# Two 16-point steps in sixteen 32x32 tiles, the second branch in column halves, and a new instruction order, in a one-core spectral filter kernel

## Chip, core and metric

The kernel runs on one core of one Trainium2 chip. Its time is the device time of one execution in microseconds (us); the figure compared is the median over runs. Five engines take part: TensorE (PE in the profile, its weight loads PEld), VectorE (DVE), ScalarE (ACT), GpSimd (POOL) and SyncE (SP). In this kernel the last two do nothing but start DMA transfers.

## The reference: what is computed

Two branches A and B filter the same input `x` of shape (2048, 1024) in the frequency domain and are mixed row by row by a gate:

```python
x = A_x
g = sigmoid((x * gate_w).sum(-1, keepdims=True))
def branch(w_r, w_i):
    X = rfft2(x.astype(float32), axes=(-2, -1))      # 2048 rows, 1024 columns -> 513
    return irfft2(X * (w_r + 1j * w_i), s=(S, D)).astype(bfloat16)
return g * branch(A_w_r, A_w_i) + (1 - g) * branch(B_w_r, B_w_i)
```

Inputs and output are bfloat16. The forward transform is shared; the product with the weights and the way back exist once for each branch (b = 0 and b = 1).

## The kernel before, in words

The 2048-point transform of the rows is split into 128 x 16. All steps are matmuls with constant matrices, their results are copied from PSUM to bfloat16 in SBUF ("evicted") by ACT or DVE, and real symmetry is used throughout. Stage by stage, with the names that the code gives to its nodes:

- **Load.** `x` comes in eight transfers of 512 KB (two of the 16 row residues `n2` each), with the matrix `F` (512 KB), then `DM` and `SK`, all from SP.
- **fS, fT, S1, Z** (`xrows`, `stage_s1`, `stage_s1f`). DVE folds columns (sum and difference of mirrored halves), PE applies the 128-point step for each residue (8 matmuls 128x256), ACT or DVE evicts to `TV`. For the residues in `FOLD2` (10 to 15) DVE folds a second time (`f2`) and the matmuls are 128x128.
- **D, Q** (`stage_d`). The column transform: 16 steps of 8 matmuls 128x256, evicted to `RING`. Every D reads all sixteen Z.
- **S2, X** (`stage_s2`). The 16-point step on the rows. The work is cut in four quarters `sq`; one S2 is 16 matmuls in four 64x64 tiles of the array (64 rows of weights by 64 columns). Evicted to `R4`.
- **mul** (`prod`). The products with the weights: 32 DVE operations, all on 128x2052 elements. Weights come through the POOL queue.
- **I, V, turn** (`stage_i1`, `stage_iw`). The inverse 16-point step: 16 stages of 32 matmuls in 64x64 tiles (`WIDE`) or 64 matmuls in 64x32 tiles. Each stage gives two tiles V of 128x1024, and each V is moved across partitions by a DMA of 256 KB (`turn`), SBUF to SBUF, from a cell of the buffer `RING` to `TV`. The cell is free again when the DMA has landed.
- **S1A, S1B, S1H, G** (`s1inv`). The inverse 128-point step of both branches, the gate folded into its matrices (`RA`, `RB`): 16 matmuls 128x128 for each residue.
- **Di, o, u, e, y, out** (`tail`). The inverse column step, and DVE folds back: `u` (only for the pairs in `FOLD3`: 0, 2, 4, 6), `e`, `y`; then the output goes out from SP in pairs of residues.

The order of the work is fixed ahead: the nodes are numbered as the code creates them, and the string `ORDER` lists them in base 36, two characters each; `ENGS` names the engine of each entry (p, a, d, g for POOL, s for SP), `CELLS` the buffer cells. `Plan.replay` reads them, and each engine executes its own nodes in that order. Each engine waits on semaphores only for what its next node needs (`Sched`). In the order before, SP's first nodes are x rows 0-1, `F`, x rows 2-3 to 14-15, `DM`, `SK`; DVE's first `mul` is the one of quarter 1 after two Q and two X.

All matmuls are issued from line 392, DVE's two-operand work from line 395, evictions from line 417 (ACT) and 418 (DVE), DMAs from line 426, so the profile is read by tensor names and shapes.

Of the kernel before, what the change touches and what calls it, by code (L numbers as in the profile page):

```python
# [4 lines left out]
dt = mybir.dt  # L5
# [5 lines left out]
NS = 513  # L11
# [4 lines left out]
FOLD2 = (10, 12, 14)  # L16
WIDE = ((0, 0), (0, 1), (0, 2), (0, 3), (1, 3))
EARLY = (0, 1, 2, 3)
FOLD3 = (0, 2, 4, 6)
PAIRS = {"warm": 12, "S2": 16, "I1": 64, "I1W": 32, "S25": 8, "gate": 8, "zg": 4, "gm": 8}  # L20
DEPTH = ((0, 2), (2, 4), (4, 6), (6, 8), (8, 10), (10, 12), (12, 14), (14, 16))
ORDER = (
    "020b0h030c000i04010506070n0j080m090f0a0g0d0q0s0e0o0t0r0k0y0w0p0z0u0l24140x15100v251b12111a181h131g1c19261o1e1p1d16271q1f"
    "1r2s28171w1s1u1i1t292v1x1v1j2a1z1m2w1k1y2t2b1n1l22202c232u212y2x2z2d3o3m2e3p3b3n2f3s3c2g3q3t372h3r31382i403u3239422j412q"
    "303v3a33352k343w3x362l493z3y2m434a3d5n3g2n445p3e3i2o473h3f45482p5o3j464o5q3k4p4b3l4h4i4j4e4c5b4f4k4d4g4l5w2r5c5r5x635z59"
    "4q5u4m774r5y644n5i605s5v5a5t4y5l4s6v5j5m4t614u4z5k6a6w50624v6d6b4x6e7n4w6c5d6h655e6f5g5f6i55665h516g56676t686j527o696o6m"
    "6u6k6n7z6r6l6x816p6s7l6q726y82706z7m757188737976747p788b8c7a7s897q7t7b808a7r57837c7e7d587f7g86538454877j857u7h7k7i8u7v7x"
    "8d7w8z7y8i908v918j8w8e8k928x8f938l8y8g8m9b94958h979f969c9u8n8o9g9q988q9v9d9r9h9e9w8p9i9s99a59x8r9a9ja99t9k8saia69l8t9yam"
    "aa9z9ma7aja09nabana1aka89oaoac9palava2apazaeawa3b8aqb0a4axadb9arbab1afaybdasbmb2agatbbahbeb4boaubcbibrbhbnb3bsbfbpbgb5bq"
    "bvb6bub7btbjbwbkbxblbybz")  # L30
ENGS = (
    "sadsadpsasssdasdsasaspdspdapdpadpagdadpagdpadpdadpagdpdapgdadpgadppdagpdadgdpapdagdappgdpappagppgdpagpdgpapgapdgpddpagds"
    "ppappgddpagpdagpaddpgadpagpdapagdpapdaaddpadppdapadapsdpadadpapdagdapgagdgpaddagpdaagpdadpadagdagpdpadagdpagpdagdapadgpa"
    "dagdagpdagdgpadasdagpadgspdagdadagpdgsdpadsdgpadadgagpagspadpspgpppapdpappadpapapddadpdapddapddapdpapdapdpadsdpaddpadsdp"
    "addpaddpadpadpdsapdapdadpdaspdadapdapdpaddpsadasadpdadadpddadddsdddddsds")
CELLS = (
    "071052794002440d28404702486402463204060846204g62402640g027420648g02461204260204406624gij7062402062446086002462460284602a"
    "0244668c026042a264680402ac60402046400824264002c406408248a060424c0460280g424078064867c60046")
# [6 lines left out]


def spot(m):
    r = m // 2
    return 32 * (m % 2) + 4 * (r % 8) + r // 8


def make_consts():
# [4 lines left out]
    for j in range(4):  # L57
        for i in range(4):
            for ri in range(2):
                for sq in range(4):  # L60
                    p = 32 * j + 8 * i + 4 * ri + sq
                    slot, at0 = 4 * sq + j % 2 * 2 + i // 2, j // 2 == 0
                    kap[p], img[p] = 32 if slot == 0 and at0 and i % 2 else 64 * (i % 2) + 16 * (j // 2) + slot, ri
# [22 lines left out]
    for par in range(2):  # L86
        for h in range(2):
            l = (2 * (2 * np.arange(128) + h) + par)[:, None]
# [31 lines left out]
    SK = np.zeros((128, 1152))  # L120
    KI = KI.reshape(2, 2, 2, 32, 32)
    for z in range(2):
        lut = []
        for b in range(2):
            for t in range(16):
                lut.append((2 * (2 * t + b),) + ((0, 1, 2 * t + b) if z else (b, 0, 2 * t)))
                lut.append((2 * (2 * t + (b if z else 1 - b)) + 1, 1 if z else b, 0, (2 * t + b) if z else 2 * t + 1))
        for hh in range(2):
            if hh:
                lut = [(4 * t + 2 * b, b, 0, 2 * t) for b in range(2) for t in range(16)] + \  # L130
                      [(4 * t + 2 * (1 - b) + 1, b, 0, 2 * t + 1) for b in range(2) for t in range(16)]
            for m, blk, y, r in lut:
                m = spot(m)
                for t in range(3):
                    SK[64 * hh + 32 * blk:64 * hh + 32 * blk + 32, z * 192 + t * 64 + m] = S2[y, t, :, r]
                for c in range(2):
                    for t, v in enumerate((KI[y, c, 0], -KI[y, c, 0], KI[y, c, 1])):
                        o = 384 + z * 384 + (c * 3 + t) * 64 + 32 * blk
                        for th in range(2):
                            SK[64 * hh + m, o + th:o + 32:2] = v[r].reshape(2, 16)[:, 8 * th:8 * th + 8].ravel()  # L140
# [8 lines left out]
    for i in range(2):  # L149
        M[64 * i:64 * i + 64, 20 + i] = 1.0  # L150
# [142 lines left out]
class Plan:  # L293
# [40 lines left out]
    def emit(self, S):  # L334
        def phys(k):
            if isinstance(k, tuple) and isinstance(k[0], Tile):
                t = k[0]
                a = self.limit[t.pool][0]
# [12 lines left out]
def bass_gated_mix__spectral_gfnet__spectral_gfnet__prompt_kernel(  # L351
# [11 lines left out]
    def ap(t, off, dims, p0=0, np_=128):  # L363
# [7 lines left out]
    SK = sb("SK", 1152)  # L371
# [3 lines left out]
    NCELL = 28  # L375
# [9 lines left out]
             {"ps": ("ps", 4), "p1": ("ps", 8), "st": ("ring", 4), "q": ("ring", 2), "qx": ("ring", 2), "v": ("ring", 14),  # L385
              "o": ("late", 8), "e": ("late", 8), "y": ("ring", 5), "u": ("ring", 5), "w": ("ring", 1)})
    xv = A_x[0].rearrange("(p r) d -> p r d", r=16)
    outv = out[0].rearrange("(p r) d -> p r d", r=16)
    wsrc = {0: (A_w_r, A_w_i), 1: (B_w_r, B_w_i)}

# [6 lines left out]
    def cost(ns):  # L397
        o = sum(max(0.056, n / 2400 + 0.0025) if n > 64 else 0.03 for n in ns)
        return {"pe": (o, o + 0.21)}

    def vt(n):
        return {"dve": (0.07 + 0.00052 * n, 0.205 + 0.00052 * n)}

    def pe(name, ns, build, reads, writes, alloc=(), **kw):
        return P.add(name, cost(ns), lambda e: build(), reads, writes, alloc=alloc, **kw)

    def ev(name, n, io, reads, writes, slow=False, only=None, **kw):
        x = 0.285 if slow else 0.0
        engs = {"act": (0.062 + 0.000833 * n + x, 0.24 + 0.000833 * n + x),
                "dve": (0.075 + 0.00104 * n + 0.08 * (x > 0), 0.22 + 0.00104 * n + 0.08 * (x > 0))}  # L410
        if only:
            engs = {only: engs[only]}

        def build(eng):
            o, i = io()
            if eng == "act":
                return [lambda e: e.activation(o, i, ACT.Copy)]  # L417
            return [lambda e: e.tensor_copy(o, i)]  # L418
        return P.add(name, engs, build, reads, writes, **kw)

    def dma(name, eng, pairs, mb, rate, reads, writes, kind=True, n=1, **kw):
        if not isinstance(eng, str):
            es = {"pool": (0.6, mb / 118 * 1000), "sp": (0.63, mb / 118 * 1000)}
        else:
            es = {eng: (0.6 * n, mb / rate * 1000)}
        n = P.add(name, es, lambda e: [lambda q, d=d, s=s: q.dma_start(d, s) for d, s in pairs()], reads, writes, dma=kind, **kw)  # L426
        n.mb = mb
        return n
# [9 lines left out]
    def cload(eng, t, off, key, a, b, keys, more=(), **kw):  # L438
        dma("c_" + key, eng, lambda: [(ap(t, off, [[1, b - a]]).bitcast(dt.uint16), cst[key].ap()[:, a:b])],
            (b - a) * 256e-6, 400, list(more), keys, **kw)  # L440

    P.add("zero8", {"dve": (0.1, 0.2)}, lambda e: [lambda e: e.memset(ap(G8, 0, [[1, 8]]), 0.0)], [], ["G8"])
    P.add("table", {"act": (1.4, 1.5)}, lambda e: [lambda e: e.activation(ap(ZG, 0, [[1, 8]]), ap(G8, 0, [[1, 8]]), ACT.Sigmoid)],
          ["G8"], ["ZG"])

    def xload(a, b):
        dma("x", "sp", lambda: [(ap(WAB, XO + a * 1024, [[1024, b - a], [1, 1024]]), xv[:, a:b, :])],
            (b - a) * 0.262, 410, [], [("x", i) for i in range(a, b)] + [("xl", a)])
# [5 lines left out]
    dma("gw", "act", lambda: [(ap(GW, 0, [[1, 1024]], 0, 1), gate_w.rearrange("(o d) -> o d", o=1))], 0.002, 400, [], ["gw"])  # L454
    cload("act", MS, 0, "MS", 0, 64, ["MS"])
    cload("sp", DM, 0, "DM", 0, 2048, ["DM"])
    cload("sp", SK, 0, "SK", 0, 1152, ["SK"])

    P.key = ("in", 1)
    pt = pit[id(WAB)]  # L460

    def rows(b, c, p, step, s0, r0, dims):
        src = wsrc[b][c]
        return (AP(WAB, p * pt + (2 * b + c) * WH + s0 * WP, [[step * pt, 32 // step]] + [[WP, d[1]] for d in dims if d[0] < 0] + [[1, dims[-1][1]]]),
                AP(src.tensor, src.offset + r0 * NS, dims))

    def wload(name, key, eng, prs, mb, b):
        dma(name, eng, lambda: prs, mb, 106, [("xl", m) for m in range(0, 8 if name in ("Ws0", "W00") else 14, 2)], [("W", b) + key], after=[("x", m) for m in range(16)] if b else [], n=len(prs))

    wk = {0: [], 1: []}  # L470

    for i, (a, b) in enumerate(((0, 256), (256, 1280))):
        P.key = ("in", 1)
        P.add("FN", {"act": (0.15 + (b - a) * 0.00083, 0.25 + (b - a) * 0.00083)},
# [398 lines left out]
```

## Time and profile before

| what | value |
|---|---|
| median of 3 runs | 126.01 us (125.93 to 126.77) |
| span of the profiled execution | 124.9 us |
| PE, DVE, ACT, POOL busy in the span | 103.4, 99.5, 96.5, 41.6 us |
| DMA moved | 27.85 MB, mean 223 GB/s |
| granted TensorE clock, mean | 0.968 |

The profiled execution has no time of its own beside its span; the 1.1 us between span and median are taken as what lies around it. How to read the views: a timeline row is start, length, engine, source line, operation, output<-input, tile, shape and count, and in brackets the idle time before it and who ended it. A window row gives for each engine the busy us and, in brackets, the instructions in that stretch, then the granted clock, the mean busy share of the 16 DMA engines and GB/s.

### The profile page before, as it was taken

How to read it: one execution, taken by the hardware profiler on the slowest of the kernel's cores; microseconds unless marked ns; L12 is line 12 of the kernel's file. 1: busy time of each engine (PE TensorE's matmuls, PEld its weight loads, DVE VectorE, ACT ScalarE, POOL GpSimd, SP SyncE). 2: the span in 40 equal slices, each digit the busy share in tenths (PEclk: the TensorE clock that was granted, in tenths of full speed). 3: DMA queues.
4: the chain of work that ended last, by engine and by line, in shares of the span. 5: the costliest groups of instructions: out<-in, count | busy, mean ns of one | idle time of the engine just before them, and what ended most of it. 6: DMA issues, size and time to landing. Idle time of an engine off the chain costs nothing.

```text
span 124.9 us, 3644 instructions
## 1 busy us (share of the span) xinstructions
PE 103.4 (83%) x1588; PEld 71.7 (57%) x1588; DVE 99.5 (80%) x134; ACT 96.5 (77%) x111; POOL 41.6 (33%) x74
## 2 busy tenths in 40 slices
PE   6799979999999999785969965896499999999610
PEld 2288836977764556333524322432389999999400
DVE  0479999458699997999999999480307899999991
ACT  4499999466999879994989695673519999999930
POOL 0007699999990003613334331333100000000000
PEclk9999999999999999999999999999859999999975
DMA  4999999999999972898675789889680004444456
GB/s 106 407 419 411 385 336 235 341 338 322 321 293 293 247 212 58 227 168 199 183 182 160 172 205 259 219 190 225 203 243 7 0 5 168 168 173 168 198 220 253
DMA packets 10881, 27.85 MB, mean 223 GB/s; under 512 B 4305, under 2 KB 4305, under 8 KB 10610
## 3 DMA queue, kind: packets, MB, share of 16 engines
q0 software_dynamic: 6688, 15.25, 45.2%
q1 hardware_dynamic: 4032, 12.36, 28.2%
q8 instruction: 12, 0.20, 0.6%
q10 hardware_dynamic: 146, 0.02, 0.1%
q14 instruction: 3, 0.02, 0.1%
HBM read 15.01 MB, written 4.19 MB: 154 GB/s over the span
## 4 chain that ended last, share of the span: by engine, by line
DVE 33%; DMA 22%; PE 22%; ACT 14%; issue 5%; SPq 1%; DVEq 0%; ACTq 0%
PE PS L392 22%; DMA TV<-RING 18%; DVE RING L395 18%; ACT RING L417 9%; DVE WAB L395 9%; DMA WAB<-in_A_x_dram 4%; DVE R L418 3%; ACT R L417 2%; DVE TV L395 2%; DVE RING L418 1%; ACT TV L417 1%; ACT FM L729 1%; ACT WAB L417 1%; SPq L426 1%; DVE WAB L418 0%
## 5 line engine op out<-in xcount | busy, mean ns | idle before, releaser
L417 ACT ACTIVATE RING<-PS 128x1024 bf16<-128x1024 f32 x41 | 40.2, 1026 | 15.0 <-PE PS L392 8.2
L395 DVE TENSOR_TENSOR WAB<-R,WAB 128x2052 bf16<-128x2052 bf16 x24 | 28.1, 1225 | 0.7 <-DMA WAB<-in_B_w_i_dram 0.6
L395 DVE TENSOR_TENSOR RING<-WAB 128x1024 bf16<-128x1024 bf16 (+1 forms) x42 | 23.9, 608 | 5.3 <-DMA WAB<-in_A_x_dram 4.5
L417 ACT ACTIVATE R<-PS 128x1024 bf16<-128x1024 f32 (+2 forms) x29 | 24.6, 937 | 4.3 <-PE PS L392 4.2
L426 POOL DMA_DIRECT2D TV<-RING x26 | 15.2, 586 | 37.1 <-ACT RING L417 20.2
L392 PE MATMUL PS<-WAB,SK 64*32 64x512 bf16 (+1 forms) x576 | 23.4, 377 | 3.4 <-ACT RING L417 3.4
L392 PEld LDWEIGHTS PS<-WAB,SK 64*32 64x32 bf16 (+1 forms) x576 | 10.5, 97 | 15.0 <-ACT RING L417 6.2
L392 PE MATMUL PS<-FM,TV 128*128 128x128 bf16 x128 | 14.5, 237 | 3.1 <-ACT RING L417 3.1
L392 PE MATMUL PS<-DM,TV 128*128 128x256 bf16 x128 | 15.5, 274 | 0.3 <-ACT TV L417 0.3
L392 PEld LDWEIGHTS PS<-FM,TV 128*128 128x128 bf16 x128 | 13.6, 120 | 3.8 <-ACT RING L417 3.8
L418 DVE CAST RING<-PS 128x1024 bf16<-128x1024 f32 x7 | 8.6, 1223 | 9.0 <-PE PS L392 4.9
L418 DVE CAST R<-PS 128x1024 bf16<-128x1024 f32 (+1 forms) x9 | 9.9, 1105 | 6.6 <-PE PS L392 6.5
L392 PEld LDWEIGHTS PS<-DM,TV 128*128 128x128 bf16 x128 | 13.3, 115 | 2.3 <-issue 1.2
L417 ACT ACTIVATE WAB<-PS 128x1024 bf16<-128x1024 f32 (+1 forms) x16 | 14.5, 1014 | 0.2 <-PE PS L392 0.2
L392 PE MATMUL PS<-DI,R 128*128 128x256 bf16 (+1 forms) x128 | 13.4, 260 | 1.1 <-ACT R L417 1.1
L417 ACT ACTIVATE TV<-PS 128x1024 bf16<-128x1024 f32 x14 | 13.3, 1040 | 0.5 <-PE PS L392 0.5
L392 PE MATMUL PS<-TV,RING 128*128 128x256 bf16 (+1 forms) x128 | 12.3, 253 | 1.7 <-DVE RING L395 0.8
L392 PE MATMUL PS<-RM,TV 128*128 128x128 bf16 x128 | 13.4, 222 | 0.0
L392 PEld LDWEIGHTS PS<-RM,TV 128*128 128x128 bf16 x128 | 12.9, 115 | 0.0
L392 PEld LDWEIGHTS PS<-TV,RING 128*128 128x128 bf16 x128 | 10.3, 98 | 4.3 <-DVE RING L395 2.2
L392 PEld LDWEIGHTS PS<-DI,R 128*128 128x128 bf16 x128 | 11.0, 98 | 2.6 <-ACT R L417 1.6
L392 PE MATMUL PS<-TV,SK 64*64 64x512 bf16 x128 | 8.4, 381 | 4.4 <-DVE RING L418 1.8
(41 smaller groups left out, 97.9 us busy)
## 6 DMA issues: line engine op xcount, KB each, us to landing
TV<-RING POOLq DMA_DIRECT2D x26, 256.0 KB, 6.0
WAB<-in_A_x_dram SPq DMA_DIRECT2D x8, 512.0 KB, 7.3
out_dram<-RING SPq DMA_DIRECT2D x7, 512.0 KB, 2.6
TV<-RING SPq DMA_DIRECT2D x6, 256.0 KB, 6.0
WAB<-in_A_w_r_dram POOLq DMA_DIRECT2D x2, 513.0 KB, 9.8
WAB<-in_A_w_i_dram POOLq DMA_DIRECT2D x2, 513.0 KB, 9.0
WAB<-in_B_w_r_dram POOLq DMA_DIRECT2D x2, 513.0 KB, 8.7
WAB<-in_B_w_i_dram POOLq DMA_DIRECT2D x2, 513.0 KB, 12.1
```

Source lines behind the costliest of these rows:

```text
L392: return lambda e: e.matmul(o, l, r, start=start, stop=stop, skip_group_check=True)
L395: return lambda e: e.tensor_tensor(out=o, in0=a, in1=b, op=op)
L417: return [lambda e: e.activation(o, i, ACT.Copy)]
L418: return [lambda e: e.tensor_copy(o, i)]
L426: n = P.add(name, es, lambda e: [lambda q, d=d, s=s: q.dma_start(d, s) for d, s in pairs()], reads, writes, dma=kind, **kw)
L729: P.add("sig", {"act": (0.92, 1.12)}, lambda e, f=f, t=t: [lambda e: e.activation(f, psl(t, 0, [[1, 1024]]), ACT.Sigmoid)], [(t,)], [("gr" ...
```

## The change

- **Frequencies dealt anew** (`make_consts`): rows are placed on partitions so that the 16-point steps become 32x32 blocks. S2 is 32 matmuls 32x512 in sixteen tiles instead of 16 in four. I is 64 matmuls 32x512 for branch 0, and for branch 1, where one stage holds one half of the columns, 128 matmuls 32x256. `SK` shrinks from 1152 to 576 columns, and the weights are cut in fewer, larger transfers, half of them on SP.
- **Branch 1 in halves of the columns**: `prod` and I of branch 1 work on columns 0-256 and 257-512 apart, the inverse 128-point step is a `half` (SI, 16 matmuls for a pair of residues and one column half) with its own G. A G needs branch 0 and its half of branch 1 alone. The `mul` still number 32.
- **turn**: each V goes out as two DMAs of 128 KB, on SP or POOL, with rows of 512 elements to 8 partitions; before, one DMA with rows of 1024 elements to 8 or 16 partitions.
- **No FOLD2, no FOLD3**: all S1 and Di have 128x256 matmuls; `f2` and `u` are gone.
- **ORDER, ENGS, CELLS** are new.

The core of the diff:

```diff
-FOLD2 = (10, 12, 14)
-WIDE = ((0, 0), (0, 1), (0, 2), (0, 3), (1, 3))
-FOLD3 = (0, 2, 4, 6)
+FOLD2 = ()
 ORDER = (
-    "020b0h030c000i04010506070n0j080m090f0a0g0d0q0s0e0o0t0r0k0y0w0p0z0u0l24140x15100v251b12111a181h131g1c19261o1e1p1d16271q1f"
...
+    "0a02080e0903050406071y200d2125231z0h000m0n0i0b0j0c010f0o0s0t0g0k0q0p0w0u0y0l0z0r0x14151a12161813100v191g1h1b17111k1l1c1e"
...
-                    for k in range(2):
-                        for i in range(2):
-                            for j in range(2):
-                                w = 192 * (sq == i == j == k == 0) + ((0, 2), (1, 0))[c][m] * 64
-                                f.append(mm(psl(t[k], i * 512 + m, [[1, 512 - m]], 64 * j, 64), ap(SK, w, [[1, 64]], 64 * i, 64),
...
+                    for j in range(4):
+                        for i in range(4):
+                            w = 96 * (sq == i == j == 0) + ((0, 2), (1, 0))[c][m] * 32
+                            f.append(mm(psl(t[i // 2], i % 2 * 512 + m, [[1, 512 - m]], 32 * j, 32), ap(SK, w, [[1, 32]], 32 * i, 32),
...
+                for c in (g,) if b == 0 else (0, 1):
+                    for i in range(4):
+                        T, off = ploc(b, pr // 2, pr % 2, 4 * sq + i)
+                        for j in range(4):
+                            w = 192 + 192 * (sq == i == j == 0) + (c * 3 + (0, 1, 2, 2)[pr]) * 32
+                            oc, n = (0, 512) if b == 0 else (c * 256, 256)
+                            f.append(mm(psl(t[j // 2], j % 2 * 512 + oc, [[1, n]], 32 * i, 32), ap(SK, w, [[1, 32]], 32 * j, 32),
+                                        ap(T, off + c + (256 * g if b else 0), [[1, n]], 32 * j, 32), pr == 0 and not oc, pr == 3))
...
+            def pairs(J=J):
+                base, st = (16384 + g * 8192, 512) if b else (g * 512, 1024)
+                return [(AP(TV, (64 * J + 32 * k + sq) * pt + base, [[4 * pt, 8], [st, 16], [1, 512]]),
+                         rg(v[J], k * 512, [[1, 512]])) for k in range(2)]
+            dma("turn", ANY, pairs, [(v[J], 0, 2)], [("V", b, sq, g, J)], after=old)
...
+    def half(ns, hf):
...
+        vk = [("V", 0, sq, g, J) for sq in range(4) for g in range(2) for J in range(2)] + \
+             [("V", 1, sq, hf, J) for sq in range(4) for J in range(2)] + [(x, ns[0] // 8) for x in ("RA", "RB")]
+        pe("SI%d" % k, lambda: [m for r, n2 in enumerate(ns) for m in s1inv(n2, t, r, hf)], vk, [(t,)], alloc=[t])
```

Read through the numbering of the nodes (2 to 10 are x rows 0-1, `F`, x rows 2-3 ... 14-15; 14 is `SK`, 13 `DM`), the new order says, engine by engine:

- SP: x rows 14-15, x 0-1, x 10-11, `SK`, x 12-13, `F`, x 4-5, x 2-3, x 6-7, x 8-9, then weights, `DM`, weights, `RM`, and turns.
- PE: S1 of residues 0, 1, 3, 2, 5, 6, 7, 4, 11, 8, 9, 10, 14, 12, 15, 13, two gate steps, then D; the first S2 after seven D, the first I after all sixteen D; the last I is the one of branch 1, quarter 1, half 1; then eight SI of half 0, and eight SI of half 1 between sixteen Di.
- DVE: folds of x 0-1, 2-3, 4-5, 6-7 first; the first `mul` (quarter 0) after three Q and two X; between the first and the last `mul` stand two Q, one V, two X and three of the four RA/RB; after it one V, the last RB, six G of half 0, one G of half 1, one `o`, and then `e` and `y`.
- ACT: 13 Z, 11 Q, 12 X, 30 V, 9 G (two of half 0) and 15 `o`.
- turns: 17 on SP, 15 on POOL; the last two V (branch 1, quarter 1, half 1) both go out on POOL.

More of the change, by code (lines that the diff above doesn't have):

```diff
@@ L395, in tt, with pe, dv, ac @@
         return lambda e: e.tensor_tensor(out=o, in0=a, in1=b, op=op)
[L397 to L412, printed above, removed]
+    def pe(name, build, reads, writes, alloc=(), **kw):
+        return P.add(name, ("pe",), lambda e: build(), reads, writes, alloc=alloc, **kw)
+    def dv(name, build, reads, writes, **kw):
+        return P.add(name, ("dve",), lambda e: build(), reads, writes, **kw)
+    def ac(name, build, reads, writes, **kw):
+        return P.add(name, ("act",), lambda e: build(), reads, writes, **kw)
+    def ev(name, io, reads, writes, engs=EV, **kw):
         def build(eng):
@@ L463, in rows, with weights @@
+    def weights(b, lo0, hi, c, kind):
         src = wsrc[b][c]
[L464 to L468, printed above, removed]
@@ L473, in bass_gated_mix__spectral_gfnet__spectral_gfnet__prompt_kernel @@
+        dma("W", ("sp", "pool")[kind], lambda: prs, [("xl", m) for m in range(0, 14 if b or lo0 or c else 8, 2)], [("W", b, lo0, c, kind)],
+            after=[("x", m) for m in range(16)] if b else [])
+        for h in range(2):
+            if lo0 < 8 * h + 8 and hi > 8 * h:
+                wk.setdefault((b, h), []).append(("W", b, lo0, c, kind))
+    for i, (a, b) in enumerate(((0, 256), (256, 2048 if not FOLD2 else 128 * FOLD2[0]))):
         P.key = ("in", 1)
-        P.add("FN", {"act": (0.15 + (b - a) * 0.00083, 0.25 + (b - a) * 0.00083)},
-              lambda e, a=a, b=b: [lambda e: e.activation(ap(TV, FO + 2048 + a, [[1, b - a]]), ap(TV, FO + a, [[1, b - a]]), ACT.Copy, scale=-1.0)],
-              ["F"], [("FN", "FN1")[i]])
+        ac("FN%d" % i, lambda a=a, b=b: [lambda e: e.activation(ap(TV, FO + 2048 + a, [[1, b - a]]), ap(TV, FO + a, [[1, b - a]]), ACT.Copy, scale=-1.0)],
+           ["F"], [("FN", "FN1")[i]])
@@ L837, in bass_gated_mix__spectral_gfnet__spectral_gfnet__prompt_kernel @@
+        dma("out%d" % k, "sp", lambda: [(outv[:, ns[0]:ns[0] + k, :], rg(y, 0, [d, [1, 1024]]))], yc, [], kind="out")
+    two = [(i, i + 1) for i in range(0, 16, 2)]
+    for hf in range(2):
+        for ns in two:
+            half(ns, hf)
+    for ns in two[:-1] + [(14,), (15,)]:
         tail(ns)
```

433 lines of the change are left out of this document (173 added, 260 removed).

## The prediction

> **What bounds the kernel now.** I read the time by stages first, then the chain of waits for the seams between them, then the timelines of DVE, ACT and PE around each seam. These windows (us; busy us with instruction counts for PE, PEld, DVE, ACT, POOL; clock; DMA share; GB/s) cut the span where one stage hands over to the next:
>
> ```profile
> 22.00:33.60 11.60, 11.54 (x132) 9.49 (x133) 6.91 (x10) 7.51 (x9) 11.60 (x21) 1.00 1.03 333
> 33.60:78.10 44.50, 36.81 (x670) 19.45 (x668) 43.79 (x43) 37.29 (x42) 15.11 (x26) 1.00 0.81 206
> 78.10:92.50 14.40, 10.70 (x256) 6.24 (x257) 4.97 (x7) 7.34 (x8) 3.96 (x7) 0.90 0.85 218
> 92.50:125.00 32.50, 25.58 (x355) 23.73 (x352) 27.48 (x52) 26.13 (x32) 0.00 (x0) 0.92 0.36 138
> ```
>
> Each stage has its own limit. From 22 to 33.6 PE is full (11.54 of 11.60): D and the first S2. From 33.6 to 78.1 DVE is full (43.79 of 44.50): the 32 `mul`. From 78 to 92.5 neither DVE (4.97) nor ACT (7.34) is: the turns are what is waited for, DMA 0.85 busy. The last 32.5 us are the way back, ACT and DVE both near full. So PE, with the largest busy time of all, sets the pace in one stage only, and most of what sixteen tiles save lies beside DVE's products.
>
> The seams, from the timelines:
>
> ```profile
> 4.24 1.29 DVE L395 TENSOR_TENSOR RING<-WAB 128x1024 bf16<-128x1024 bf16 x2 [3.10 <-DMA WAB<-in_A_x_dram]
> 5.69 1.36 ACT L475 ACTIVATE TV<-TV 128x256 bf16<-128x256 bf16 x2 [1.56 <-DMA TV<-c_F]
> 6.99 3.33 DVE L395 TENSOR_TENSOR RING<-WAB 128x1024 bf16<-128x1024 bf16 x5 [1.45 <-DMA WAB<-in_A_x_dram]
> 8.34 7.16 PE L392 MATMUL PS<-TV,RING 128*128 128x256 bf16 x64
> 22.06 5.40 PE L392 MATMUL PS<-DM,TV 128*128 128x256 bf16 x48 [0.35 <-ACT TV L417]
> 33.64 2.37 DVE L395 TENSOR_TENSOR TV<-R,WAB 128x2052 bf16<-128x2052 bf16 x2
> 60.82 15.03 DVE L395 TENSOR_TENSOR WAB<-R,WAB 128x2052 bf16<-128x2052 bf16 x13
> 76.90 1.22 DVE L395 TENSOR_TENSOR WAB<-R,WAB 128x2052 bf16<-128x2052 bf16 x1
> 92.54 2.20 PE L392 MATMUL PS<-RM,TV 128*128 128x128 bf16 x32
> 121.13 1.21 DVE L395 TENSOR_TENSOR RING<-WAB 128x512 bf16<-128x512 bf16 x3
> ```
>
> I write the path as five terms, before: start to the first D 22.1; first D to first `mul` 11.6; first to last `mul` 44.4 (33.64 to 78.1); last `mul` to the inverse step of branch 1 (S1B at 92.54) 14.4; from there to the end 32.4. Sum 124.9.
>
> **Term 1, the head: +5.3.** The three 512-KB transfers at the front of SP's queue let their readers go at 4.24, 5.69 and 6.99, that is one every 1.3 to 1.45 us in the order in which they were issued. The new order puts x 14-15, x 0-1, x 10-11, `SK` (half as large now, 147 KB) and x 12-13 ahead of `F`, and x 4-5 ahead of x 2-3. With 1.3 us each: x 0-1 at 5.5, `F` at 9.8 instead of 5.7, x 2-3 at 12.4, x 6-7 at 13.7, x 8-9 at 15.0. S1 of residues 0 and 1 can run from about 10.2, and then PE waits for x 2-3 and its two folds (1.29): 13.7. From there fourteen residues of 8 matmuls 128x256 remain, for without FOLD2 none is 128x128 any more; at 7.16/64 = 0.11 us each that is 12.3 us, to 26.0. ACT's last Z (1.0) and the hand-over put the first D at 27.4. The six `f2` that go (0.6 us each on DVE) bring nothing here, since DVE is then waiting for x. Were the eight transfers not served in turn, this term would fall back to about zero; it is a rival below. PE is idle from the end of its warm-up matmuls to 10.2; a lower clock in the first two residues falls into the wait for x 2-3.
>
> **Term 2, first D to first `mul`: -1.5.** Before `mul` stand eight D (0.88 each, 7.0), two S2, gate work of about 0.6 and an X. How long an S2 or an I lasts in sixteen tiles is not in the trace; the nearest rows are these:
>
> ```profile
> 69.78 1.93 PE L392 MATMUL PS<-WAB,SK 64*32 64x512 bf16 x64 [0.19 <-ACT RING L417]
> 42.97 1.06 PE L392 MATMUL PS<-TV,SK 64*64 64x512 bf16 x16
> 20.73 0.25 PE L392 MATMUL PS<-MS,FM 128*128 128x1 bf16 x4
> L392 PE MATMUL PS<-WAB,SK 64*32 64x512 bf16 x384 | 11.5, 377 | 2.1 <-ACT RING L417 2.1
> L392 PE MATMUL PS<-MS,FM 128*128 128x1 bf16 x16 | 1.0, 166 | 0.0
> ```
>
> The last two rows give the mean of one such matmul in ns. Four with one column take 0.25 us where one takes 0.166: three more starts in 0.084, 28 ns apart, with full weight loads between them. The first: 64 matmuls in eight tiles are eight rounds. One matmul lasts 0.377, so seven rounds take 1.55, 0.222 each, and a 512-column round alone is 0.228 in the second row ((1.06 - 0.377)/3). So eight starts with small weight loads cost a round nothing that shows; what is left for them is a few ns each. Bounds: 16 starts cost nothing beyond the round (0.22), or 28 ns each (0.45). I take the first, because the row is the same instruction with the next tile size. Then S2 is 2 rounds, 0.45 instead of 0.89; I of branch 0 is 4 rounds, 0.89 instead of 1.77, and of branch 1 eight half rounds, 0.89. 7.0 + 0.9 + 0.6 + 0.15 + X and hand-over 1.4 = 10.1, first `mul` at 37.5.
>
> **Term 3, the products: +0.5.**
>
> ```profile
> 44.95 5.61 ACT L417 ACTIVATE RING<-PS 128x1024 bf16<-128x1024 f32 x6 [0.86 <-PE PS L392]
> 48.21 3.51 DVE L395 TENSOR_TENSOR WAB<-R,WAB 128x2052 bf16<-128x2052 bf16 x3 [0.64 <-DMA WAB<-in_B_w_i_dram]
> ```
>
> DVE does 32 `mul` at 15.03 less 0.09 over 13, about 1.14, = 36.4, five evictions between them (1.14, the same spacing) 5.7, three RA/RB 1.8, small ones 0.3: 44.2. I add the 0.7 that DVE lost in the same stage before: 44.9, last `mul` at 82.4. PE has some 36 us of work here in 55 (D 14, S2 3.6, I 14, gates and the rest 4), so the 17 us that the tiles save on S2 and I end as idle time. ACT has from 47 on 30 V, six X and two sigmoids, 38 at 0.94 (5.61/6): 36 us, to 83; it keeps up without slack. Before, DVE waited for the weights of branch 1 until 48.2; they may come some 4 us later now, behind x, and are first asked for near 52. POOL's 32 weight DMAs (0.6 us each, from 15) and SP's are issued before the first turn. No cost taken, up to 2 us above.
>
> **Term 4, last `mul` to the last turn: -4.5.** These rows show what held the stage:
>
> ```profile
> ACT RING L417 <- DMA TV<-RING: 6.6, 7, 1.8
> DVE RING L418 <- DMA TV<-RING: 4.1, 1, 4.1
> 82.06 7.63 DMA TV<-RING
> TV<-RING POOLq DMA_DIRECT2D x26, 256.0 KB, 6.0
> TV<-RING SPq DMA_DIRECT2D x6, 256.0 KB, 6.0
> L426 POOL DMA_DIRECT2D TV<-RING x26 | 15.2, 586 | 37.1 <-ACT RING L417 20.2
> L418 DVE CAST RING<-PS 128x1024 bf16<-128x1024 f32 x7 | 8.6, 1223 | 9.0 <-PE PS L392 4.9
> ```
>
> Evictions wait for cells whose turn has not landed: five stages of I were still to come after the last `mul`. In the new order only one is. It takes PE 0.9 + 0.2, DVE 1.2 for its V, and POOL four issues at 0.59 (two a V now) with the last of them near 85.5; a turn lands a median of 6 us after its issue: 92.3, 9.9 after the last `mul`. Nothing is queued on POOL behind these; the eight SI of half 0 and their G (six on DVE, 6.9 us; two on ACT) fill this time, and `RB` with them.
>
> Can the transfers keep up? The first turn goes out near 48.5, as before, and 32 of them at 0.262 MB and 218 GB/s are 1.20 us each, 38.5 us: from 50.5 to 89. By the bounds of the trace it is 1.20 (both queues, 78 to 92.5) or 1.46 (48 to 62, POOL alone, row below). I take 1.20 since both queues are used again.
>
> ```profile
> 48.00:62.00 14.00, 11.01 (x189) 5.57 (x187) 13.79 (x14) 11.76 (x14) 5.62 (x10) 1.00 0.78 180
> 97.00:112.00 15.00, 15.00 (x224) 14.45 (x222) 14.72 (x27) 15.00 (x18) 0.00 (x0) 1.00 0.27 107
> 98.00 0.22 PE L392 MATMUL PS<-FM,TV 128*128 128x128 bf16 x1
> 98.89 0.22 PE L392 MATMUL PS<-FM,TV 128*128 128x128 bf16 x1
> 112.56 1.89 DVE L395 TENSOR_TENSOR WAB<-WAB 128x1024 bf16<-128x1024 bf16 x3
> L395 DVE TENSOR_TENSOR RING<-WAB 128x512 bf16<-128x512 bf16 x12 | 4.6, 418 | 0.6 <-ACT WAB L417 0.6
> out_dram<-RING SPq DMA_DIRECT2D x7, 512.0 KB, 2.6
> ```
>
> **Term 5, the tail: -3.5.** From the last turn PE has eight SI and sixteen Di. 16 matmuls 128x128 are 0.89 (98.00 to 98.89), 8 of 128x256 are 0.88: 24 x 0.89 = 21.3. ACT evicts 22 of them at 0.94, 20.7, beside it; from 97 to 112 both ran without a gap. The last `o` is there at 0.1 + 21.3 + 0.2 + 1.0 = 22.6. Then five folds at 0.6 (three in 1.89), and from there 0.1 to issue, 2.6 to land and 0.5 to the span's end, 28.9 after the last turn, 121.2. Dropping `u` (eight operations of 0.42) and eight G done ahead is what shortens it; the Di that get wider cost PE 32 x 0.055 = 1.8, which is in the 21.3.
>
> Sum: 124.9 + 5.3 - 1.5 + 0.5 - 4.5 - 3.5 = 121.2; with the 1.1 us between span and median **122.3**.
>
> **The rivals.**
>
> *The turns become the bound (slower).* Each turn is now two DMAs of 128 rows of 1 KB instead of one of 2 KB rows, each to 8 partitions. For it: the DMA engines were 0.85 busy at only 218 GB/s, far from the 333 of the loads, and the 8-partition turns of branch 0 went at 180. Against it: all turns may use both queues, and the two halves of one write to different partitions. It decides from 1.29 us per turn (50.5 + 32c + 0.5 > 92.3); from 1.41 the whole gain is gone (last turn at 96). At 1.46 the end is 127.7; if 1-KB rows cost 1.6 us a turn, 102.2 + 28.9 + 1.1 = 132. Twice the cost of today (the row count, 2.4) would be over 150. I take 132 for it.
>
> [...] No view of before separates the engines, so the chance rests on the 180 GB/s.
>
> *The head costs nothing.* If x arrived in the new order without PE waiting, 5.3 us less: 117.0. Three readers released in issue order speak against it.
>
> *Sixteen tiles do not run together.* With 28 ns between starts an I of branch 1 takes 128 x 0.028 = 3.6 us, of branch 0 1.8, an S2 0.9: PE then has 14 + 7.2 + 43 + 4 = 68 us for the 55, and the stage ends 13 us later: 135. [...]
>
> *DVE and ACT hold each other up* in a middle stage where neither has slack: 3 to 5 us, 125 to 128.
>
> **How the numbers follow.** Forecast (120 to 125) 0.45; turns 0.28, of which 0.1 beyond 134; head free 0.13; tiles 0.04; ACT and DVE 0.10. Range: 117.0 takes in the free head, 134 all but the far end of the turns. Over 1% is what this measurement tells from no change: faster means below 124.75: 0.38 + 0.13 = 0.51; within 1% 0.15 (the upper edge of the forecast, half of the last rival, a little of the turns); slower 0.34.
>
> **What would show it.** In the profile after: PE's first S1 near 10 and first D near 27; 64 matmuls 32x512 in about 1.1 us with the drain, 128 of 32x256 in about the same; 32 `mul` without gaps from 37 to 82; S2 and I busy on PE halved; the last turn landing near 92 with SI of half 0 before it; ACT full from there to 115. What would make it wrong: a first D near 22; evictions that wait for turns for much longer than the 10.7 us of before in all; DMA below 200 GB/s from 50 to 90.

## The result, and the profile after

The changed kernel takes 159.91 us (median of 4 runs, 159.65 to 161.98) beside 125.97 for the kernel before (125.18 to 126.77): 1.2716 times as long, 95% interval 1.2609 to 1.2823. The forecast was 122.3 us in a range of 117 to 134. It was wrong in sign and far in size.

Lines of the page after: span, busy us and instructions of each engine, and from its list of DMA queues (packets, MB, share of the 16 engines) one that the prediction did not read:

```profile
span 157.7 us, 5569 instructions
...
PE 111.0 (70%) x2548; PEld 83.4 (53%) x2548; DVE 98.6 (63%) x120; ACT 95.5 (61%) x104; POOL 35.3 (22%) x66
...
PEclk9975899999959985555567765555558999999995
...
q8 instruction: 20, 0.33, 0.9%
```

DVE and ACT do the same work as before in nearly the same time (98.6 and 95.5 us busy, before 99.5 and 96.5). TensorE has 2548 matmuls with their weight loads where it had 1588. In the line `q8 instruction` 20 packets in 0.33 MB are 16.5 KB each (16384 bytes each in the trace), and 2 x 2548 instructions over 20 are 255. I read it so that this queue brings TensorE's own program in blocks of 256 instructions, which makes 64 bytes for an instruction; the counts of the runs below agree. The page before has the line too:

```profile
q8 instruction: 12, 0.20, 0.6%
```

That is 2 x 1588 / 256 = 12.4 blocks. What the engines waited for after the change (us in total, times, longest):

```profile
PEld PS L373 <- issue: 28.4, 32, 4.5
...
ACT RING L391 <- PE PS L373: 22.3, 16, 3.9
...
PE PS L373 <- issue: 17.8, 8, 4.1
...
ACT RING L391 <- DMA TV<-RING: 2.1, 1, 2.1
```

And POOL's turns (count, KB each, median us from issue to landing):

```profile
TV<-RING POOLq DMA_DIRECT2D x30, 128.0 KB, 4.1
```

Before, ACT's evictions to `RING` waited 6.6 us for turns and 8.2 for TensorE; now 2.1 and 22.3. TensorE in turn waits on "issue", that is on nothing that the profile shows of another engine. In the chain of waits "issue" holds 14% of the span (before, 5%), and a stretch of it looks like this (start, length, what):

```profile
93.59 2.64 issue
96.23 2.01 PE PS L373 x118
98.24 1.54 issue
99.78 2.02 PE PS L373 x123
101.80 1.53 issue
```

The same place in TensorE's timeline, and two S2 earlier that are torn:

```profile
54.94 0.61 PE L373 MATMUL PS<-RING,SK 32*32 32x512 bf16 x21 [0.74 <-ACT RING L391]
59.62 1.49 PE L373 MATMUL PS<-RING,SK 32*32 32x511 bf16 x43 [4.06 <-issue]
...
96.23 2.01 PE L373 MATMUL PS<-WAB,SK 32*32 32x256 bf16 x127 [2.64 <-issue]
99.78 2.02 PE L373 MATMUL PS<-WAB,SK 32*32 32x256 bf16 x128 [1.54 <-issue]
103.33 2.07 PE L373 MATMUL PS<-WAB,SK 32*32 32x256 bf16 x127 [1.53 <-issue]
```

The two S2 (64 matmuls) are torn after the 21st for 4.06 us, in the middle of a stage, whose inputs are all there before its first matmul. From 96 to 107 a stage of branch 1 (128 matmuls with 128 weight loads: 256 instructions, one block) starts every 3.55 us, of which it runs 2.0 and waits 1.5. That is 27.7 ns for a matmul with its weight load, 13.9 ns for an instruction.

The trace also holds the times of the packets of `q8`. Two of them start at 97.46 and 101.02 us and take 0.92 and 0.96. Each starts about 1.24 us after TensorE began its current block (96.23, 99.78), and TensorE begins the next one about 1.37 us after the packet's end (99.78, 103.33). So only about a quarter of the 3.55 us is the transfer itself, and in this stretch the packet of the next block starts only after TensorE has begun the present one.

By the terms of the prediction, with a run that is told below (half of the accumulation left out) beside them:

| from, to | before | forecast | after | half work |
|---|---|---|---|---|
| start, first D | 22.1 | 27.4 | 29.1 | 28.6 |
| first D, first `mul` | 11.6 | 10.1 | 12.8 | 14.4 |
| first to last `mul` | 44.4 | 44.9 | 57.9 | 47.2 |
| last `mul`, end | 46.8 | 38.8 | 57.9 | 49.4 |
| span | 124.9 | 121.2 | 157.7 | 139.5 |

The column of after comes from these rows, first of TensorE's timeline, then of DVE's:

```profile
10.63 1.89 PE L373 MATMUL PS<-TV,RING 128*128 128x256 bf16 x8 [4.14 <-ACT TV L453]
...
12.75 15.22 PE L373 MATMUL PS<-TV,RING 128*128 128x256 bf16 x120
...
29.09 6.30 PE L373 MATMUL PS<-DM,TV 128*128 128x256 bf16 x56
```

```profile
41.87 1.23 DVE L376 TENSOR_TENSOR TV<-R,WAB 128x2052 bf16<-128x2052 bf16 x1 [2.11 <-issue]
...
98.56 1.23 DVE L376 TENSOR_TENSOR WAB<-R,WAB 128x2048 bf16<-128x2048 bf16 x1
...
113.91 1.22 DVE L392 CAST RING<-PS 128x1024 bf16<-128x1024 f32 x1 [14.11 <-PE PS L373]
```

The last shows where the end goes: DVE idles 14 us for the last inverse steps, which TensorE still issues block by block long after the last product.

### The profile page after: what moved, and what is told of

It reads as the page before. It is cut to its first block, busy times and chain, and to the rows that moved or that the text cites. A ratio compares the mean times of both kernels' runs of the same rounds, so it can differ in the third digit from the quotient of the medians.

```text
span 157.7 us, 5569 instructions
## 1 busy us (share of the span) xinstructions
PE 111.0 (70%) x2548; PEld 83.4 (53%) x2548; DVE 98.6 (63%) x120; ACT 95.5 (61%) x104; POOL 35.3 (22%) x66
## 4 chain that ended last, share of the span: by engine, by line
PE 48%; ACT 22%; issue 14%; DVE 8%; DMA 4%; SPq 2%; DVEq 0%
PE PS L373 48%; ACT RING L391 9%; ACT WAB L391 6%; ACT R L391 5%; DMA TV<-c_F 4%; DVE R L392 3%; DVE WAB L376 2%; DVE RING L376 2%; SPq L397 2%; DVE RING L392 1%; ACT TV L391 1%; ACT FM L684 1%; DVE FM L376 0%; ACT TV L453 0%; DVEq L233 0%
## 5 line engine op out<-in xcount | busy, mean ns | idle before, releaser
L391 ACT ACTIVATE RING<-PS 128x1024 bf16<-128x1024 f32 x41 | 39.8, 1024 | 24.4 <-PE PS L373 22.3
L373 PE MATMUL PS<-WAB,SK 32*32 32x256 bf16 (+1 forms) x1280 | 24.8, 411 | 16.1 <-issue 11.5
L391 ACT ACTIVATE R<-PS 128x1024 bf16<-128x1024 f32 (+1 forms) x24 | 21.9, 943 | 16.3 <-PE PS L373 16.3
L376 DVE TENSOR_TENSOR WAB<-R,WAB 128x2052 bf16<-128x2052 bf16 (+2 forms) x24 | 28.7, 1227 | 3.4 <-PE PS L373 3.2
L373 PEld LDWEIGHTS PS<-WAB,SK 32*32 32x32 bf16 x1280 | 17.9, 95 | 21.8 <-issue 16.2
L376 DVE TENSOR_TENSOR RING<-WAB 128x1024 bf16<-128x1024 bf16 (+1 forms) x34 | 20.9, 656 | 11.6 <-DMA WAB<-in_A_x_dram 10.3
L392 DVE CAST R<-PS 128x1024 bf16<-128x1024 f32 (+1 forms) x12 | 13.4, 1136 | 12.9 <-PE PS L373 12.8
L373 PE MATMUL PS<-TV,RING 128*128 128x256 bf16 x128 | 17.1, 303 | 4.1 <-ACT TV L453 4.1
L373 PEld LDWEIGHTS PS<-TV,RING 128*128 128x128 bf16 x128 | 13.7, 108 | 7.7 <-ACT TV L453 5.0
L373 PE MATMUL PS<-RM,TV 128*128 128x128 bf16 x128 | 17.1, 233 | 0.0
L391 ACT ACTIVATE WAB<-PS 128x1024 bf16<-128x1024 f32 x15 | 15.0, 1123 | 2.8 <-PE PS L373 2.8
L373 PE MATMUL PS<-DM,TV 128*128 128x256 bf16 x128 | 15.9, 284 | 0.1
L373 PE MATMUL PS<-RING,SK 32*32 32x512 bf16 (+2 forms) x288 | 8.9, 470 | 8.8 <-issue 6.2
L373 PE MATMUL PS<-DI,R 128*128 128x256 bf16 x128 | 15.0, 273 | 0.0
L373 PEld LDWEIGHTS PS<-RM,TV 128*128 128x128 bf16 x128 | 13.5, 105 | 0.0
```

The source lines that it names most:

```text
L373: return lambda e: e.matmul(o, l, r, start=start, stop=stop, skip_group_check=True)
L376: return lambda e: e.tensor_tensor(out=o, in0=a, in1=b, op=op)
```

## Experiments

Theory F (fetch): TensorE can use up blocks of its program faster than they come, about one per 3.55 us; sixteen tiles and half columns need more instructions for the same columns. Theory C (clock): the granted clock fell to about half in the middle, and that makes the stages slow. Theory T: the turns. And the order itself, head and end, may be slow whatever TensorE does.

**Half the instructions, the same streaming.** In branch 1 one matmul reads 256 columns twice and writes 512, in place of two:

```diff
-                for c in (g,) if b == 0 else (0, 1):
+                for c in (g,) if b == 0 else (0,):
...
-                            oc, n = (0, 512) if b == 0 else (c * 256, 256)
+                            dims = [[1, 512]] if b == 0 else [[0, 2], [1, 256]]
...
```

> Changed kernel, but each stage of branch 1's inverse 16-point step issues 64 matmuls of 512 columns (the 256 columns read twice; the second output half is therefore not the reference's) instead of 128 of 256: the same streaming on PE, 512 pairs of weight load and matmul fewer (1024 instructions, four blocks of 16 KB). Fetch theory (PE waits for its own instructions, 256 at a time, about 3.5 us a block): no idle 'issue' gaps between these stages, 11 to 18 us less, 142 to 149 us. Clock theory (PE is slow because it is granted half its clock in this stretch): the same streaming at the same clock, within 2 us of 159.9. Turn theory (transfers of V are the bound): within 2 us of 159.9.

149.28 us (145.53 to 150.35): 10.6 less for 1024 instructions less, just past the upper edge of F's range; C and T expected no change. Three waits of 0.5 to 0.9 us are left in the last stages of branch 1, where F expected none.

**Twice the instructions, the same streaming.** Each matmul of branch 1 is cut in two of 128 columns:

```diff
-                            oc, n = (0, 512) if b == 0 else (c * 256, 256)
-                            f.append(mm(...
+                            oc, n = (0, 512) if b == 0 else (c * 256, 128)
+                            for z in range(1 if b == 0 else 2):
+                                f.append(mm(psl(t[j // 2], j % 2 * 512 + oc + 128 * z, ...
```

> Changed kernel, each matmul of branch 1's inverse 16-point step split in two of 128 columns: the same streaming and the same result, 1024 pairs more (2048 instructions, eight blocks). Fetch theory: 3 to 3.5 us for each block more, 184 to 190 us, a stage of branch 1 every 7 us. Clock theory and turn theory: within 3 us of 159.9.

189.95 us (187.34 to 191.39), 30.0 more for 2048 instructions: 14.7 ns each, close to the 13.9 of the timeline. TensorE's waits go with the count. The rows of waits of the half-count run and of the double run:

```profile
PE PS L373 <- issue: 8.1, 8, 3.2
```

```profile
PE PS L373 <- issue: 35.7, 17, 4.3
```

8.1, 17.8 and 35.7 us of waiting; the pages count 16, 20 and 28 blocks (2 x 2036, 2548 and 3572 instructions over 256 are 15.9, 19.9 and 27.9).

**The kernel before, its 16-point matmuls cut in two.** All columns in halves, the tiles and the order as before:

```diff
-    f.append(mm(psl(t[j], c * 512, [[1, 512]], ...), ..., pr == 0, pr == 3))
+    for z in range(2):
+        f.append(mm(psl(t[j], c * 512 + 256 * z, [[1, 256]], ...), ..., pr == 0 and z == 0, pr == 3))
```

> Kernel before, each matmul of its two 16-point steps (64x64 and 64x32 tiles) split in two column halves: the same streaming, tiles, transfers and order, 832 pairs more (1664 instructions, 6.5 blocks); 1664 matmuls in the two steps, where the changed kernel has 1792. Fetch theory: idle 'issue' gaps of 1 to 2.5 us in the 16-point stages, 134 to 146 us. Clock theory (the cause is the short work of the sixteen tiles): no more than 2 us above 126.

139.7 us beside 127.37 for the kernel before, 1.1003 times as long (1.0704 to 1.1302). So it is neither the 32x32 tiles nor the new order that bring the waits: more instructions for the same columns do it in the kernel before as well.

Its row of waits, which the kernel before does not have for matmuls (its weight loads waited 0.4 us at most):

```profile
PE PS L392 <- issue: 15.8, 9, 3.1
```

**Fillers that keep the clock up.**

```diff
-            f = []
+            f = [mm(psl(t[0], 0, [[1, 512]]), ap(DM, 0, [[1, 128]]), ap(DM, 0, [[1, 512]]), True, True)] * (8 * b)
```

> Eight extra 128x512 matmuls stand at the head of each of the eight stages of branch 1; the stage's own first matmuls overwrite what they write, so the output is that of the changed kernel. Fetch theory (PE waits for blocks of its own instructions): the blocks still come one per 3.55 us, a stage has 272 instructions instead of 256, so the eight stages cost 0.2 us more each and the fillers fit in the time PE waits: 159 to 163 us, with the granted clock in the middle higher and the stage's own matmuls shorter than 2.0 us. Clock theory (the stages are slow because PE idles and is granted half the clock): with PE kept busy the 256 own instructions take 1.0 us and the fillers 1.7, 2.7 in place of 3.55, and branch 0 gains too: 148 to 154.

161.27 us (160.3 to 162.67). The windows from 60 to 120 us of the changed kernel, then of this run:

```profile
60.00:80.00 20.00, 14.36 (x603) 8.60 (x587) 17.45 (x18) 14.03 (x17) 3.54 (x6) 0.50 0.39 108
80.00:100.00 20.00, 11.56 (x583) 8.07 (x559) 16.32 (x16) 13.01 (x14) 7.07 (x12) 0.67 0.69 190
100.00:120.00 20.00, 11.86 (x471) 9.97 (x440) 3.00 (x3) 6.88 (x8) 4.74 (x8) 0.52 0.42 124
```

```profile
60.00:80.00 20.00, 15.12 (x585) 8.43 (x560) 16.18 (x17) 13.01 (x16) 3.54 (x6) 0.76 0.35 100
80.00:100.00 20.00, 13.80 (x480) 8.28 (x484) 16.19 (x16) 12.32 (x14) 7.07 (x12) 0.83 0.61 179
100.00:120.00 20.00, 14.56 (x567) 8.91 (x569) 3.06 (x4) 8.22 (x9) 4.73 (x8) 1.00 0.40 118
```

The clock went from 0.50, 0.67, 0.52 to 0.76, 0.83, 1.00, the 64 fillers of 512 columns stream on top, and the time stays: theory C falls. In these stages the 128 matmuls of a stage now take 1.7 to 1.9 us and its eight fillers 1.7, so TensorE is nearly full and the time alone would not say what it waits for. The run also shows what the waits are tied to. A stage now has 136 matmuls, a block still 128 (TensorE's timeline, the fillers left out):

```profile
97.19 0.83 PE L373 MATMUL PS<-WAB,SK 32*32 32x256 bf16 x63
98.55 0.86 PE L373 MATMUL PS<-WAB,SK 32*32 32x256 bf16 x65 [0.53 <-issue]
...
101.17 0.76 PE L373 MATMUL PS<-WAB,SK 32*32 32x256 bf16 x54
102.12 0.95 PE L373 MATMUL PS<-WAB,SK 32*32 32x256 bf16 x74 [0.19 <-issue]
...
104.84 0.69 PE L373 MATMUL PS<-WAB,SK 32*32 32x256 bf16 x46
105.95 1.20 PE L373 MATMUL PS<-WAB,SK 32*32 32x256 bf16 x82 [0.42 <-issue]
```

The wait falls after 63, 54 and 46 of a stage's own matmuls: it moves by 8 or 9 from stage to stage, as the boundary of a block does, and each lasts until a new block is due (98.55, 102.12, 105.95).

**Half the work.** One of two passes in S2, two of four in I are left out, `for pr in (0, 3)`; every eviction, product and turn stays.

> In every sixteen-tile stage one half of the accumulation is left out (one of two passes in S2, two of four in IA and IB), so the output differs; every wait, eviction, product and transfer stays. Pairs: 2548 - 128 - 256 - 512 = 1652, against 1588 in the kernel before. Fetch theory: PE's waits on its own instructions fall from 17.8 us to under 3, the clock comes back, and 134 to 142 us are left; the excess over the kernel before is then head (first product at 41.9 against 33.6) and tail. Rival (the new order itself is what is slow, whatever TensorE does): 147 or more, hardly under the 149.3 of the half-count run.

142.17 us (139.61 to 143.84), 1.1166 times the kernel before (1.1035 to 1.1297): just past the upper edge of F's range. TensorE's matmuls show no wait on issue any more, and DVE is full (45.00 of 47.17 us in the first window below, first to last product; the second goes to the end). The stage takes 47.2 us where 44.9 were forecast. Streaming and count are both halved here; that it is the count that tells rests on the run with half the instructions and the same streaming. One expectation of F failed: the clock did not come back, it is 0.58 in the first window, with no matmul waiting on issue. Here a low clock is therefore no sign of these waits. 16 us over the kernel before are left.

```profile
42.95:90.12 47.17, 27.92 (x864) 16.64 (x864) 45.00 (x43) 38.01 (x43) 14.18 (x24) 0.58 0.82 206
90.12:139.50 49.38, 32.89 (x480) 29.68 (x457) 31.77 (x46) 26.64 (x29) 3.55 (x6) 0.81 0.40 137
```

One of its waits is used below:

```profile
PE PS L373 <- DMA TV<-RING: 3.6, 1, 3.6
```

**The head.** First x and `F` in turn (first tokens of `ORDER`, full work):

```diff
-    "0a02080e0903050406071y200d2125231z
+    "02030405060708090a0e1y200d2125231z
```

> Changed kernel, the first ten transfers of SP put back in the order x 0-1, F, x 2-3 ... x 14-15, SK; nothing else. If the queue serves them in turn: first D 4.5 to 5.5 us earlier (near 24) and 153 to 157 us. If the order of the loads is hidden anyway: first D near 29, 159 to 161 us.

160.19 us (156.99 to 162.92): no gain in the median. The first D comes 3.7 us earlier than after the change (expected were 4.5 to 5.5), for TensorE now waits for `DM`:

```profile
25.44 6.28 PE L373 MATMUL PS<-DM,TV 128*128 128x256 bf16 x56 [2.90 <-DMA DM<-c_DM]
```

Then also the last of the four pieces of weights that the first product needs (`1z`), moved from fourth to second in POOL's queue:

```diff
-...1y200d2125231z
+...1y200d211z2523
```

> x0 to x7 and F in turn, and the fourth piece of the first weights second instead of fourth in POOL's queue. The first product, which began at 41.87 as that piece landed (41.79), should begin at 36 to 38. If the middle only shifts with it: 154 to 157 us. If the instruction stream sets when the inverse steps end, whenever the first product comes: 158 to 161.

159.24 us (155.35 to 162.13): the median is 0.7 under the kernel after, two of the four runs are under its lowest (159.65) and two over its median. The first product in DVE's timeline, with x in turn and then with the piece moved:

```profile
42.78 1.23 DVE L376 TENSOR_TENSOR TV<-R,WAB 128x2052 bf16<-128x2052 bf16 x1 [6.70 <-issue]
```

```profile
38.50 1.23 DVE L376 TENSOR_TENSOR TV<-R,WAB 128x2052 bf16<-128x2052 bf16 x1
```

With x in turn alone DVE was ready 6.7 us before the weights were; with the piece moved it does not wait, and begins 3.4 us earlier than after the change (41.87). In the profiled execution, the slowest of the four, nothing of it arrives at the end: the first final stage (SI) starts at 117.09, after the change at 115.19. That fits the blocks of TensorE's program setting when the inverse steps are over. Whether the two quicker runs gained 3 to 4 us from the head is not shown; the last run of this section, which holds the same head, gains nothing.

**Half the work and the head together.**

> The half-work run and the head run in one kernel. If head and instruction stream are the two causes and add: 4 to 6 us under the half-work run, 129 to 137. If something else in the order holds the middle (products, turns, evictions): within 2 us of the half-work run.

144.19 us (142.63 to 147.96), 2.0 above the half-work run: that the two causes add is not borne out. The first product came at 38.40, but the last at 89.81, no earlier than in the half-work run (88.90). Two rows of its waits say what came instead:

```profile
ACT RING L391 <- DMA TV<-RING: 11.0, 2, 7.7
...
DVE WAB L376 <- DMA WAB<-in_B_w_i_dram: 7.2, 1, 7.2
```

The first turns go out earlier, at 50.6, but land only at 59 to 63, as late as the last pieces of the weights (59.7 to 61.0): ACT waits 7.7 us for a cell, and DVE, which does the products, waits 7.2 us for weights of branch 1.

**The weights in longer runs.** The run before with POOL's half of the weights read forward in runs of n rows, in place of single rows backwards (those rows then hold the wrong frequencies):

```diff
-..., [[2 * pt, 16], [WP, n], [1, NS]], [[128 * NS, 16], [-NS, n], [1, NS]]))
+..., [[2 * pt, 16], [1, n * NS]], [[128 * NS, 16], [1, n * NS]]))
```

> The run with half work and head, and POOL's half of the weights read in runs of n x 1026 bytes instead of single reversed rows of 1026 (the same bytes and transfers; the order of those rows is left wrong, and half of each accumulation is left out as before). In the run with half work and head the first turns, issued at 50.6, landed at 59 to 63 behind the last pieces of the weights (59.7 to 61.0), and ACT waited 7.7 us for a ring cell. Theory W (the redealt weights move at about 230 GB/s where the kernel before had 300, because of their single rows, and hold up the turns): the weights end at 50 to 54, ACT's wait goes, 136 to 140 us in place of 144.2. Rival (the rate comes from something else, the rows or the queues): weights at about 60 again, 142 to 146.

141.63 us (138.74 to 142.27), between the two expectations. ACT's longest wait fell from 7.7 to 4.4 us and DVE's wait for the weights from 7.2 to 3.7, and the rate from 35 to 45 us rose only from 209 to 245 GB/s; in the kernel before it is 278 in the same window. The rows are a part of it. What else slows the redealt weights stays open.

**One turn past another.** Two entries of SP's queue change about, on top of that run:

```diff
-...777w75...
+...77757w...
```

> The run before, with two turns of SP's queue changed about: the last turn of the first half of branch 1 ahead of a turn of the second half. In the half-work run the first final stage waited 3.6 us for that turn, issued at 91.59 behind the other. If the queue's order is what held the final stages: 2 to 4 us under the wide-weights run. If something else is as late (the last inverse step stands ahead of the final stages on TensorE anyway): within 1 us of it.

138.23 us (134.06 to 139.3), 3.4 less, as expected if the queue's order held up the final stages. In the half-work run's chain the place is this:

```profile
90.54 1.01 SPq L397
91.59 4.79 DMA TV<-RING
...
103.47 1.24 DVE R L392
...
106.75 3.50 DVE R L392 x3
```

The first final stage starts at 96.47, when a turn of half 0 lands that SP issued at 91.59, behind one of half 1. In the run with the swap TensorE no longer waits for a turn there: its first final stage starts at 94.38, in the run without at 97.03. The order held it up, by somewhat less than the medians say: in the profiled executions the first product came 2.8 us earlier with the swap (35.29, without 38.07), though nothing ahead of it was changed, and the last product 0.6 earlier.

**The kernel before with half of its 16-point work.** The ceiling of what sixteen tiles could save:

> The kernel before with half of the accumulation of each 16-point stage left out (one of two passes in S2, two of four in both forms of I), so the output differs; evictions, products, turns and order stay. It is about what sixteen tiles could save on TensorE at best, with no instruction added. Theory of the prediction (the products on DVE and the turns set the middle, TensorE's streaming is hidden beside them): 122 to 126 us, so the most that the change could have won is 0 to 4 us. Rival (TensorE's 16-point steps are on the path): 116 to 121.

126.4 us (121.94 to 128.19) beside 125.24 (123.48 to 128.77). Leaving out half of TensorE's 16-point work in the kernel before gains nothing that can be told from the spread; the fastest runs of the two are 1.5 us apart.

**Both repairs of the order, full work.**

> The changed kernel, whole and with its full computation, with both repairs of the order that the shortened runs pointed to: x, F and the first weights in turn, and the last turn of the first half ahead of one of the second. Fetch theory: the first product comes 3 to 6 us earlier, but TensorE's blocks still end the inverse steps near 114, and the final stages start behind them: 157 to 160 us. If the repairs add to what they gave with half the instructions (0 and 3 us), or pass on the earlier start: 152 to 156.

161.64 us (158.94 to 162.39), 1.288 times the kernel before (1.2714 to 1.3046): no gain, and 1.6 us over what F expected. Its first product began at 37.07, 4.8 us earlier than after the change, and its first final stage at 116.19, 1.0 later (after the change 115.19). None of these versions is faster than the kernel before.

## Why the prediction was wrong

**The step that failed** is the price of a matmul in a small tile: "16 starts cost nothing beyond the round", taken from a row with eight tiles. As streaming it was right for 512 columns:

```profile
51.75 0.65 PE L373 MATMUL PS<-TV,SK 32*32 32x512 bf16 x32
52.20 0.69 PE L373 MATMUL PS<-WAB,SK 32*32 32x512 bf16 x32
```

The second row starts 0.45 us after the first, whose 32 matmuls are two rounds: 0.45, as forecast. With 256 columns it was a little short: in the filler run two stages of branch 1 ran through without a wait, their 128 matmuls in 1.45 and 1.56 us, the second in a window with a clock of 1.00, where about 1.1 was forecast. What was never counted is the program. An S2 went from 16 matmuls to 32, an I of branch 0 from 32 to 64, of branch 1 from 64 (quarter 3: 32) to 128. In all 960 more, 1920 instructions; at 13.9 ns each they ask for 26.7 us. In the sum for the products, S2 and I stood with 3.6 and 14 us of TensorE; their 1792 matmuls at 27.7 ns would ask for 49.6. The eight-tile I in the quoted row of before used 128 instructions in 1.93 us, 15.1 ns each, just above the 13.9 at which blocks come. Twice as many tiles at the same width streamed twice as fast (32 matmuls of 512 columns in 0.45 us, where eight tiles needed four rounds of 0.22), and blocks that come at 13.9 ns an instruction left no room for that.

In the kernel before, whose program comes in 12 such blocks, weight loads waited 0.4 us at most on issue; after the change the eight waits of TensorE's matmuls on issue lasted 1.5 to 4.1 us.

**A rival with the right price for another reason.** "Sixteen tiles do not run together" set 28 ns a start and 3.6 us a stage of branch 1; measured were 27.7 and 3.55. Its mechanism is refuted: within a block 128 matmuls ran in 2.0 us at a clock of 0.50, 16 ns apart, and 65 in 0.86 us in the filler run, 13 ns. It had a chance of 0.04, and its 135 us counted what the middle loses to it but not what the end does.

**The head: right in size, in part by luck.** S1 began at 10.63 (forecast 10.2), the first D at 29.1 (27.4). But the forecast had TensorE wait for x 2-3 until 13.7 and then run 112 matmuls at 0.11 us, and said that a lower clock "falls into the wait". There was no such wait: the first eight matmuls took 1.89 us, 0.24 each, the other 120 followed in 15.22 us, and the clock line has 7 and 5 tenths from 8 to 16 us. The low clock took the place of the wait and 1.7 us more. With x in turn the first D came 3.7 us earlier and the median did not move.

**First D to first `mul`: wrong by 2.7.** "No cost taken" for the weights looked at branch 1. What was late is a piece of branch 0's first quarter, fourth in POOL's queue; the head runs show it.

**The products: +0.5 forecast, +13.5 measured.** 10.7 of it go with half the work; DVE's own row then has 45.00 of 47.17 busy, 2.3 over the forecast. That "the 17 us that the tiles save on S2 and I end as idle time" is borne out by the halved run of the kernel before: there was next to nothing to win there.

**The turns: not the bound, as forecast.** POOL's median from issue to landing fell from 6.0 to 4.1 us with two DMAs a turn, and ACT's wait for cells from 6.6 to 2.1. After the change the turns are spread over a longer time (first to last issue 54.9 to 117.0 us, before 48.8 to 90.8), which makes this easy; but in the half-work run, whose products take 47.2 us, ACT waited only 2.0 us for cells as well. The page gives no landing for SP's turns, and two of them in that run's chain took 4.8 and 6.9 us.

**The last two terms: forecast 38.8, measured 57.9.** 8.5 of the 19.1 go with half of the 16-point work (49.4). For the other 10.6 the step "the eight SI of half 0 and their G ... fill this time" failed. In the half-work run the last inverse step ends at 92.85, 2.7 us after the last product, but the first SI starts at 96.47, when the late turn has landed; six of the eight G go one after another on DVE (the last two rows of the chain above are such waits), and the first Di starts at 111.20. That is 21.1 us after the last product, where the forecast has about 11 (9.9 to the last turn and one SI). The turn caught in SP's queue is only a part of it: with the two turns changed about 50.3 us lie behind the last product, without it 52.4, both in the version with the earlier head. The rest is read from the timeline and was not tried by itself.

Sum: 36.5 us lie between forecast span and span after; 18.2 are gone with half of the 16-point work, 18.3 stay, 5.5 of them up to the first product, 2.3 in the products, 10.6 behind.

## What to carry to other kernels

Count TensorE's instructions by stage beside its columns: here two for a matmul (2548 matmuls, 2548 weight loads), which took 13.9 ns each where they went on for several blocks of 256, and 14.7 by the run with 128 columns. Smaller tiles and narrower columns traded streaming for instructions, and the stage got longer from it: an I of branch 1 went from 64 matmuls in 1.93 us to 128, a stage every 3.55 us. Before making a stage faster, leave half of its work out and look whether the time moves; here that run (126.4 us beside 125.24) would have said that there was next to nothing to win.

## What the runs showed of the hardware

After the change TensorE's program came in 20 blocks of 256 instructions. Where stages used them up faster, a new one began at 96.23, 99.78, 103.33 and 107.15 us, and every 3.55 to 4.00 us from 101.86 to 131.79 in the run with twice the instructions; the engine stopped for it, in the middle of a stage too (4.06 us after the 21st of 64 matmuls). The profile calls that "issue". Of the 3.55 us about 0.94 were the packet's transfer; what fills the 1.24 before it and the 1.37 behind it stays open. From 60 to 120 us, where TensorE waited so, the granted clock was 0.50 to 0.67, and with fillers 0.76 to 1.00 at nearly the same time (161.27 us beside 159.91): the clock in that stretch was no cause. Nor was it a sign of such waits: in the half-work run, where no matmul waited on issue, it was 0.58 from the first to the last product.
